# Banded attention inside a fused attention and feed-forward kernel: local scores of two heads in one product, against keys held with zeros for the other head

## The chip, the cores and the metric

The kernel runs on one core of one Trainium2 chip. TensorE (PE) multiplies matrices out of SBUF into PSUM banks; VectorE (DVE), ScalarE (ACT) and GpSimd (POOL) do elementwise work; SyncE (SP) issues most of the DMAs. The metric is the device time of one execution in microseconds (us); a median of several runs is given.

## What is computed

Two parts, one behind the other, all in float32:

```
# q, k, v: (8 batches, 8 heads, 576 tokens, 64)
pooled: q, k, v averaged over groups of 4 tokens -> 144 x 144 softmax attention, repeated 4 times
local:  softmax over |i - j| < 4 only          -> banded attention over 576 tokens
x = pooled + local, as (4608 tokens, 512)
h = x @ w_in                 # 512 -> 2048
out = (h * cos(h)) @ w_out   # 2048 -> 512
```

The weights come as float64 and are split on the chip into a high and a low part; so are x and h * cos(h). Three products (high-high, high-low, low-high) stand for one.

## The kernel before

**Attention units.** The work of one batch and one pair of heads is a unit: 8 batches by 4 pairs, 32 units. Its pieces are `u_qk` (loads q and k of two heads, 128 partitions = two heads by 64 dimensions, and sums groups of four tokens into `qkd` for the pooled part), `u_v` (loads and sums v), `u_s` (scores, softmax), `u_t` (transposes of the probabilities) and `u_pv` (probabilities times v; the result goes as `xs` into the tiles `x0h, x0l` to `x3h, x3l`). Batches 0 and 1 (`b < NEARLY`) run at the start while weights are split, the 24 units of batches 2 to 7 between the products of the feed-forward part.

**Local scores of a unit from batch 2 on (line 539).** Tokens are cut into 24 pieces of 24 queries; a piece meets 32 keys. 4 pieces lie on the four groups of 32 partitions of a PSUM bank, 6 such columns (`NSEG`) make a head. Each of the 48 products of a unit takes the 64 rows of one head (`hs`), 32 stationary columns of q and 32 moving columns of k, and one bank per head. In the profile each float32 product is two records, so L539 has 96 records a unit. The pooled scores (line 555, 8 records) follow in the same PE operation. Then come, on DVE, the mask (`band`, line 569), the maxima (574, 582), the subtractions (399, 585), on ACT the exponentials (605, 606), on DVE the sums (610), the reciprocals (612, 614) and the scaling (616, DVE or POOL).

**Moving probabilities (line 641).** DVE transposes the local probabilities in blocks (634); four DMAs on SP then move them into `ptb`, in which the other half of every 64 rows is zero, so that line 686 (24 products, 48 records) multiplies two pieces at once. Line 650 transposes the pooled probabilities on PE, 465 or 466 copies them into `ptd`, 667 multiplies them by v.

**Feed-forward.** A step is one tile of 384 tokens by one chunk of 128 hidden columns: `gemm1` (line 741, 12 matmuls), then on ACT and DVE h * cos(h) (750 to 759), and two steps later `gemm2` (line 777, 9 matmuls). There are 12 tiles by 16 chunks, 192 steps. Tiles 0 to 2 go in four blocks of four chunks (steps 0 to 47), tiles 3 to 11 one after the other; tile 3 (step 48) is the first that needs batch 2.

**Order.** Every operation is recorded with an estimated duration and what it reads and writes; a list scheduler (`Plan`) turns this into one fixed order per engine, which the engines then follow. A buffer that is used again is a ring: a later user waits for the earlier one. `dma` records a load with a planned latency of 1.8 us. `unit(last, step, ahead, ...)` places the pieces of a unit in recording order: `u_s` at `last`, `u_t` one `step` later, `u_pv` two. Where the planner sees PE idle in the first 300 us of its plan, it puts in products of an identity (line 916) that keep PE busy.

Of the kernel before, what the change touches and what calls it, by code (L numbers as in the profile page):

```python
# [300 lines left out]
def attn_ffn_kernel(ctx: ExitStack, tc: tile.TileContext, qT, kT, vdn, vl, w_in, w_out, out):  # L301
# [24 lines left out]
    band = const.tile([P, NSEG, BS], F32, name="band")  # L326
# [56 lines left out]
    def dma(nbytes, fn, r=(), w=(), pw=()):  # L383
        def begin():
            ins = fn()
            if ins is not None and len(begun) < FIRST:
                if len(begun) >= AHEAD:
                    tc.add_manual_dep(ins.ins, begun[-AHEAD].name, mybir.DependencyInfo(
                        mybir.DependencyClass.Sync, mybir.DependencyReason.DATA), reason="loads in flight")
                begun.append(ins.ins)  # L390
        o = pl.op("SP", max(0.45, nbytes / 262e3), begin, r=r, w=w, pw=pw, lat=1.8)
        loads.setdefault((pl.name,) + pl.arg, []).append(o)
        return o
# [52 lines left out]
    def ub(b, pr, name):  # L446
        shape, n, chunk, off = UNIT[name]
        if b == 1 and pr and name in "qk":

            own = cut(xx[1], 584 * (name == "k"), shape) if pr == 1 else \  # L450
                cut(wx[{(2, "q"): ("o", 8), (2, "k"): ("i", 7), (3, "q"): ("o", 7), (3, "k"): ("o", 6)}[(pr, name)]], 0, shape)
            return own
        if b < NEARLY and pr:
            return cut(wx[OWN[5 * (NPAIR - 1 - pr) + chunk]], off, shape)
        return sb({"ptl": "sml", "xs": "vd4"}.get(name, name), 2 if name == "ptl" else n, shape)
# [13 lines left out]
    def u_qk(b, pr):  # L469
# [4 lines left out]
        bk = bank(b, "t") if early and ON_PE else None  # L474
        for i, (src, ram) in enumerate(((q, qT), (k, kT))):
            dma(4 * P * SP_, lambda src=src, ram=ram: sp.dma_start(src.get(), ram[b, pr]), w=[src])
# [33 lines left out]
    def u_s(b, pr):  # L510
# [5 lines left out]
        if b == NEARLY and pr == 0:  # L516
            zeroed.extend((pl.buf(None), pl.buf(lambda: ptb, "ptb")))

            def zero():
                pool.tensor_copy(band, mask[:, 1:2].broadcast_to([P, NSEG, BS]))  # L520
                pool.memset(band[0:BS, 0, 0:PAD], NEG)
                pool.memset(band[P - BS:P, NSEG - 1, BQ + PAD:BS], NEG)
                pool.memset(ptb, 0.0)
            pl.op("POOL", 2.5, zero, w=zeroed)
# [6 lines left out]
        def l_mm():  # L531

            if b >= NEARLY:
                for f in range(2):
                    for n in range(NSEG):
                        for g in range(4):
                            h = (g // 2 + f) % 2
                            hs, o, c = slice(64 * h, 64 * h + 64), (4 * n + g) * BQ, LQ + BS * n
                            pe.matmul(banks[h].get()[BS * g:BS * (g + 1), c:c + BS],  # L539
                                      q.get()[hs, o:o + BS], k.get()[hs, o:o + BS], start=True, stop=True)  # L540
                return
# [17 lines left out]
        else:  # L559
            pl.op("PE", 1.55, lambda: (l_mm(), d_mm()), r=[q, k, qkd], pw=banks, w=loc + poo)  # L560
# [7 lines left out]
        for h in range(2):  # L568
            using(banks[h], pl.op("DVE", _dve(NSEG * BS), lambda h=h: dve.tensor_tensor(  # L569
                out=sml.get()[:, NSEG * h:NSEG * (h + 1)], in0=banks[h].get()[:, LQ:LQ + NSEG * BS].rearrange("p (s n) -> p s n", n=BS),  # L570
                in1=mask[:, h:h + NSEG] if b < NEARLY else band, op=ALU.add), r=[loc[h]] + zeroed[:1], pw=[sml]))
# [56 lines left out]
    def u_t(b, pr):  # L628
# [7 lines left out]
        if b >= NEARLY:  # L636
# [5 lines left out]
            dma(8 * P * NSEG * BS, move, r=[ptl], w=[u["ptb"]])  # L642
# [13 lines left out]
    def u_pv(b, pr):  # L656
# [24 lines left out]
        def w_mm():  # L681
            v4, pt = vt.get().rearrange("p a i n -> p (a i) n"), u["ptb"].get()
            for n in range(NSEG):
                for e, h in ((0, 0), (1, 1), (0, 1), (1, 0)):
                    r, o = slice(64 * e, 64 * e + 64), 2 * n * BQ
                    pe.matmul(banks[e].get()[64 * h:64 * h + 64, o:o + 2 * BQ], v4[r, NSEG * h + n, :],  # L686
                              pt[r, :, NSEG * h + n, :BQ], start=True, stop=True)
# [149 lines left out]
    for b in range(2, B):  # L837
        t0, t1 = tile_of(b * S), tile_of(b * S + S - 1)
        lo, hi = (done[t1 - NX] if t1 >= NX else 0), first[t0]
        for i in range(NPAIR):  # L840

            last = max(lo - 2.5 + (hi - lo - 1.0) * i / (NPAIR - 1), last + 1.5)
            unit(last, 1.4, 2.5, b, i)
# [116 lines left out]
```

## Time and profile before

| | |
|---|---|
| median of 3 runs | 1003.04 us (1002.43, 1003.04, 1006.76) |
| profiled execution, time / span | 1007.08 us / 1005.3 us |
| PE busy | 985.1 us, 98% of the span |
| DVE / ACT / POOL busy | 678.2 / 610.2 / 223.8 us |
| chain that ended last | PE 89%, DVE 5%, DMA 1% |
| granted PE clock, mean | 0.988 |

The busy times are shares of one profiled execution; which engine sets the end in which stretch is read from the windows and the chain, not from the totals. The profiled execution took 4.0 us more than the median of the runs.

### The profile page before, as it was taken

The page shows a single profiled execution, that of the slowest core. Times are in us where ns is not written, and L with a number is a line of the kernel's source. Part 1 is how long each engine was busy: PE and PEld are TensorE (multiplying, and loading weights), DVE is VectorE, ACT ScalarE, POOL GpSimd, SP SyncE. Part 2 cuts the span into 40 slices and gives each one's busy share as a digit, 9 for nine tenths or more (in the row PEclk, how much of TensorE's full clock was granted, in tenths as well). Part 3 has the DMA queues.
Part 4 walks back from the last instruction along what each step waited for, and adds up shares of the span by engine and source line. Part 5 has one row for each costly group of instructions (what it writes and reads, how often), then busy time and mean ns, then how long its engine had stood idle before and what let it go on. Part 6 is the DMA issues. An engine that isn't in the chain of part 4 may idle for free.

```text
span 1005.3 us, 23882 instructions
## 1 busy us (share of the span) xinstructions
PE 985.1 (98%) x9932; PEld 850.3 (85%) x9932; DVE 678.2 (67%) x1362; ACT 610.2 (61%) x1174; POOL 223.8 (22%) x280
## 2 busy tenths in 40 slices
PE   8898999999998999999999999999999999999998
PEld 5556898899886888889888888888888888899997
DVE  7699999985686678464758957655657765433433
ACT  4357688876665656555547746654646665655554
POOL 6685334631242203000002211200001300000000
PEclk9699999999999999999999999999999999999999
DMA  7874733332453422210212412201112320100000
GB/s 230 250 249 159 255 119 62 72 59 45 75 131 105 84 66 70 66 33 28 82 48 71 127 49 58 82 26 36 64 52 73 116 60 4 37 1 1 32 1 32
DMA packets 41051, 80.70 MB, mean 80 GB/s; under 512 B 4976, under 2 KB 16240, under 8 KB 40944
## 3 DMA queue, kind: packets, MB, share of 16 engines
q1 hardware_dynamic: 37056, 72.11, 23.2%
q0 software_dynamic: 3888, 7.08, 5.0%
q8 instruction: 78, 1.28, 0.5%
q14 instruction: 29, 0.24, 0.1%
HBM read 57.93 MB, written 16.52 MB: 74 GB/s over the span
## 4 chain that ended last, share of the span: by engine, by line
PE 89%; DVE 5%; DMA 1%; issue 1%; ACT 1%; POOL 1%; SPq 0%; ACTq 0%; POOLq 0%; DVEq 0%
PE bank L777 38%; PE bank L741 38%; PE bank L539 2%; PE bank L916 2%; PE bank L686 2%; PE bank L555 2%; PE bank L667 2%; PE bank L650 1%; DMA q<-qT 1%; PE bank L679 1%; DVE su L610 1%; DVE xxh L421 0%; DVE tr L756 0%; PE bank L546 0%; DVE xxh L425 0%
## 5 line engine op out<-in xcount | busy, mean ns | idle before, releaser
L777 PE MATMUL bank<-wo,gh 128*128 128x512 f32 x1152 | 363.9, 397 | 0.0
L777 PEld LDWEIGHTS bank<-wo,gh 128*128 128x128 f32 x1152 | 210.2, 188 | 38.1 <-issue 3.2
L777 PE MATMUL bank<-wo,gl 128*128 128x512 f32 x576 | 227.7, 396 | 0.0
L752 ACT ACTIVATE tr<-bank,bmagic 128x384 f32<-128x384 f32 x192 | 110.9, 578 | 114.1 <-PE bank L741 109.2
L756 DVE SCALAR_TENSOR_TENSOR tr<-tr,bank 128x384 f32<-128x384 f32 x192 | 105.0, 547 | 108.1 <-ACT tr L751 107.4
L753 DVE SCALAR_TENSOR_TENSOR tr<-tr,bank 128x384 f32<-128x384 f32 x192 | 105.7, 551 | 82.8 <-ACT tr L752 81.8
L750 ACT ACTIVATE tr<-tr 128x384 f32<-128x384 f32 x192 | 100.6, 524 | 77.0 <-DVE tr L753 76.4
L758 ACT ACTIVATE gh<-tr 128x384 fp32r<-128x384 f32 x163 | 85.3, 523 | 91.9 <-DVE tr L756 90.1
L399 DVE TENSOR_TENSOR gl<-tr,gh 128x384 fp32r<-128x384 f32 x154 | 91.7, 596 | 63.5 <-ACT gh L758 59.8
L777 PEld LDWEIGHTS bank<-wo,gl 128*128 128x128 f32 x576 | 108.1, 188 | 23.5
L741 PE MATMUL bank<-x3h,wi 128*128 128x384 f32 x384 | 106.9, 338 | 1.6 <-DVE tr L756 1.0
L741 PE MATMUL bank<-x0h,wi 128*128 128x384 f32 x384 | 107.0, 339 | 0.0
L741 PE MATMUL bank<-x1h,wi 128*128 128x384 f32 x384 | 107.0, 339 | 0.0
L741 PE MATMUL bank<-x2h,wi 128*128 128x384 f32 x384 | 106.8, 339 | 0.0
L751 ACT ACTIVATE tr<-tr 128x384 f32<-128x384 f32 x192 | 100.9, 525 | 6.1
L399 POOL TENSOR_TENSOR gl<-tr,gh 128x384 fp32r<-128x384 f32 x38 | 43.3, 1139 | 268.2 <-DVE gh L759 174.7
L741 PEld LDWEIGHTS bank<-x3h,wi 128*128 128x128 f32 x384 | 70.2, 188 | 4.3 <-DVE tr L756 1.5
L741 PEld LDWEIGHTS bank<-x0h,wi 128*128 128x128 f32 x384 | 70.2, 188 | 2.4 <-DVE wxo L569 0.2
L741 PEld LDWEIGHTS bank<-x1h,wi 128*128 128x128 f32 x384 | 70.2, 188 | 2.4 <-issue 0.4
L741 PEld LDWEIGHTS bank<-x2h,wi 128*128 128x128 f32 x384 | 70.2, 188 | 2.2 <-DVE xxh L425 0.2
L741 PE MATMUL bank<-x3l,wi 128*128 128x384 f32 x192 | 64.6, 336 | 0.1
L741 PE MATMUL bank<-x0l,wi 128*128 128x384 f32 x192 | 64.5, 336 | 0.0
(199 smaller groups left out, 1457.2 us busy)
## 6 DMA issues: line engine op xcount, KB each, us to landing
vl<-vl SPq DMA_DIRECT2D x26, 384.0 KB
out<-ob SPq DMA_DIRECT2D x36, 256.0 KB
wdi<-w_in SPq DMA_DIRECT2D x16, 512.0 KB
wdo<-w_out SPq DMA_DIRECT2D x16, 512.0 KB
q<-qT SPq DMA_DIRECT2D x26, 292.0 KB
k<-kT SPq DMA_DIRECT2D x26, 292.0 KB
vd<-vdn SPq DMA_DIRECT2D x26, 288.0 KB
out<-ob POOLq DMA_DIRECT2D x27, 256.0 KB, 5.3
```

The costliest lines, as they stand in the source:

```text
L399: f = lambda e: lambda: e.tensor_tensor(out=out(), in0=in0(), in1=in1(), op=ALU.subtract)
L539: pe.matmul(banks[h].get()[BS * g:BS * (g + 1), c:c + BS], q.get()[hs, o:o + BS], k.get()[hs, o:o + BS], start=True, stop=True)
L555: pe.matmul(banks[h].get()[:HD, i * SD:(i + 1) * SD], qkd.get()[hs, 0, i * HD:(i + 1) * HD], qkd.get()[hs, 1, :], start=True, stop=True)
L667: pe.matmul(banks[0].get()[64 * h:64 * h + 64, 2 * SD:3 * SD], vd.get()[:, kh, 64 * h:64 * h + 64], ptd.get()[:, h, kh, :], start=(kh == 0 ...
L741: pe.matmul(ph.get()[:, :m], w[:, i, kc, :], x[:, kc, :], start=(n == 0), stop=(n == 3 * KC - 1))
L750: act.activation(tr.get(), tr.get(), AF.Sin, scale=PI)
L751: return act.activation(tr.get(), tr.get(), AF.Square)
L752: pl.op("ACT", _act(m, True, 1), lambda: act.activation(tr.get(), h(), AF.Identity, bias=bmagic), r=[ph], w=[tr])
L753: pl.op("DVE", _dve(m), lambda: dve.scalar_tensor_tensor(out=tr.get(), in0=tr.get(), scalar=MAGIC, in1=h(), op0=ALU.subtract, op1=ALU.subt ...
L756: pl.op("DVE", _dve(m), lambda: dve.scalar_tensor_tensor(out=tr.get(), in0=tr.get(), scalar=0.5, in1=h(), op0=ALU.subtract, op1=ALU.mult), ...
L758: pl.op("ACT", _act(m, False), lambda: act.activation(gh.get(), tr.get(), AF.Copy), r=[tr], w=[gh], alts=[("DVE", _dve(m / 2), lambda: dve ...
L777: pe.matmul(o, (gh, gh, gl)[k].get()[:, sl], wo.get()[:, (0, 1, 0)[k]], start=(c == c0 and k == 0), stop=(c == c1 - 1 and k == 2))
```

## The change

From batch 2 on, k is loaded as two DMAs of 64 partitions into one constant buffer `kz` of two planes: plane 0 has head 0 in the upper 64 partitions and zeros below, plane 1 zeros above and head 1 below. POOL writes the zeros once. A product of line 560 takes all 128 rows of q (32 stationary columns) and 2 by 32 moving columns, one piece of both heads; there are 24 in a unit instead of 48, and the columns in PSUM run by piece and head instead of by head. `band` follows that order, with two more columns and as bfloat16, and line 707 (686 before) reads the probabilities by it. The sums of k in groups of four become two DVE operations of 64 partitions each, without POOL as an alternative. `ptd` now lies in the buffer of `smd`. In the planner, the move of the probabilities has a latency of 3.4 instead of 1.8 us, the score operation costs 1.3 instead of 1.55, units keep 2.25 instead of 1.5 steps of distance at least, and the pieces of a unit follow at 1.1 instead of 1.4 steps.

```diff
@@ constants
-    band = const.tile([P, NSEG, BS], F32, name="band")
+    band = const.tile([P, NSEG + 2, BS], BF16, name="band")
+    kz = const.tile([P, 2, SP_], F32, name="kz")
@@ ub: buffers of a unit
+        if name == "k" and (b >= NEARLY or not pr):
+            return pl.buf(lambda: kz if b >= NEARLY else kz[:, 0], "k.0")
...
-        return sb({"ptl": "sml", "xs": "vd4"}.get(name, name), 2 if name == "ptl" else n, shape)
+        return sb({"ptl": "sml", "xs": "vd4", "ptd": "smd"}.get(name, name), 2 if name == "ptl" else n, shape)
@@ u_qk
+        halves = [(slice(64 * h, 64 * h + 64), h) for h in range(2)]
+        def zero():
+            for hs, h in halves:
+                pool.memset(kz[hs, 1 - h], 0.0)
+        def load():
+            for hs, h in halves:
+                ins = sp.dma_start(kz[hs, h], kT[b, pr][hs])
+            return ins
+        def sums():
+            for hs, h in halves:
+                dve.tensor_reduce(out=qkd.get()[hs, 1], in_=kz[hs, h, PAD:PAD + S].rearrange("p (a r) -> p a r", r=4), axis=AX.X, op=ALU.add)
         for i, (src, ram) in enumerate(((q, qT), (k, kT))):
+            if i and not early:
+                if b == NEARLY and pr == 0:
+                    pl.op("POOL", 1.5, zero, w=[k])
+                dma(4 * P * SP_, load, pw=[k])
+                pl.op("DVE", 2 * _dve(S), sums, r=[k], pw=[qkd])
+                continue
@@ u_s
-                for f in range(2):
-                    for n in range(NSEG):
-                        for g in range(4):
-                            h = (g // 2 + f) % 2
-                            hs, o, c = slice(64 * h, 64 * h + 64), (4 * n + g) * BQ, LQ + BS * n
-                            pe.matmul(banks[h].get()[BS * g:BS * (g + 1), c:c + BS],
-                                      q.get()[hs, o:o + BS], k.get()[hs, o:o + BS], start=True, stop=True)
+                for n in range(NSEG):
+                    for g in range(4):
+                        o, c = (4 * n + g) * BQ, LQ + 2 * BS * (n % 3)
+                        pe.matmul(banks[n // 3].get()[BS * g:BS * (g + 1), c:c + 2 * BS].rearrange("p (h n) -> p h n", h=2),
+                                  q.get()[:, o:o + BS], k.get()[:, :, o:o + BS], start=True, stop=True)
-            pl.op("PE", 1.55, lambda: (l_mm(), d_mm()), r=[q, k, qkd], pw=banks, w=loc + poo)
+            pl.op("PE", 1.3, lambda: (l_mm(), d_mm()), r=[q, k, qkd], pw=banks, w=loc + poo)
...
-                in1=mask[:, h:h + NSEG] if b < NEARLY else band, op=ALU.add), r=[loc[h]] + zeroed[:1], pw=[sml]))
+                in1=mask[:, h:h + NSEG] if b < NEARLY else band[:, 2 * h:2 * h + NSEG], op=ALU.add), r=[loc[h]] + zeroed[:1], pw=[sml]))
@@ u_t, u_pv
-            dma(8 * P * NSEG * BS, move, r=[ptl], w=[u["ptb"]])
+            dma(8 * P * NSEG * BS, move, r=[ptl], w=[u["ptb"]], lat=3.4)
-                              pt[r, :, NSEG * h + n, :BQ], start=True, stop=True)
+                              pt[r, :, 2 * n + h, :BQ], start=True, stop=True)
@@ places of the units
-            last = max(lo - 2.5 + (hi - lo - 1.0) * i / (NPAIR - 1), last + 1.5)
-            unit(last, 1.4, 2.5, b, i)
+            last = max(lo - 2.5 + (hi - lo - 1.0) * i / (NPAIR - 1), last + 2.25)
+            unit(last, 1.1, 2.5, b, i)
```

Since the planner makes a new order, the line numbers move by 21 to 23 from `u_qk` on (741 is 762, 777 is 798, 916 is 937), and so do instructions on all engines. Three places show it.

On PE, where the feed-forward reaches tile 3 (the first matmul with `x3h`). Before, after the last product with v of batch 2 stand a whole step of tile 2 and its `gemm2`:

```order
L667 MATMUL bank<-ptd,vd 64x144 x4
L686 MATMUL bank<-ptb,vl 64x48 x24
L777 MATMUL bank<-wo_2992,gh 128x512 x2
...
L741 MATMUL bank<-x2h,wi_3176 128x384
...
L777 MATMUL bank<-wo_3090,gl 128x512
L741 MATMUL bank<-x3h,wi_932 128x384
```

Now the same product with v stands later, straight before tile 3, with six identity products (two of the twelve rows are shown) and the scores of the next unit between them:

```order
L798 MATMUL bank<-wo_2833,gl 128x512
L688 MATMUL bank<-smd,vd 64x144 x4
L707 MATMUL bank<-ptb,vl 64x48 x24
L937 LDWEIGHTS ident_b
L937 MATMUL bank<-ident_b 128x512
...
L560 MATMUL bank<-kz,q 32x64 x24
L576 MATMUL bank<-qkd 72x144 x4
L762 MATMUL bank<-x3h,wi_919 128x384
```

The last product with v of batch 2 moved from more than a step ahead of tile 3 to right ahead of it; two more identity products stand one step earlier.

On DVE at the same place, the first unit of batch 3: its mask (L569, L590), and the last unit of batch 2, whose result is added up by L698 (L719). Before:

```order
L569 TENSOR_TENSOR sml<-bank,band 128x192 x2
L582 TENSOR_REDUCE mxd<-bank 72x2
L574 TENSOR_REDUCE mxl<-sml 128x12
...
L490 TENSOR_REDUCE qkd<-q 128x144
L504 TENSOR_TENSOR vd_4137<-vd_4137 72x2x256
L505 TENSOR_TENSOR vd<-vd_4137 72x256
L466 TENSOR_SCALAR xd<-bank 128x144
L756 SCALAR_TENSOR_TENSOR tr<-tr,bank 128x384
L698 TENSOR_TENSOR vd_4248<-bank,xd 128x6x48
```

Now:

```order
L527 TENSOR_TENSOR vd_3890<-vd_3890 72x2x256
L528 TENSOR_TENSOR vd<-vd_3890 72x256
L719 TENSOR_TENSOR vd_4091<-bank,xd 128x6x48 x2
L400 TENSOR_TENSOR x3l<-vd_4091,x3h 128x384
L590 TENSOR_TENSOR sml<-bank,band 128x192 x2
...
L774 SCALAR_TENSOR_TENSOR tr<-tr,bank 128x384
L513 TENSOR_REDUCE qkd<-q 128x144
L491 TENSOR_REDUCE qkd<-kz 64x144 x2
L631 TENSOR_REDUCE su<-sml 128x12
```

The additions of the finished unit moved ahead of the next unit's mask, and the sums of q and k (now three operations) stand behind them, ahead of the softmax sums of the running unit.

On SP, the loads of the first unit of batch 3 (v is `vd_3893`, then `vd_3890`). Before:

```order
L641 DMA ptb<-sml 32x384 x4
L497 DMA vd_3893<-vdn 72x1024
L476 DMA q<-qT 128x584
L476 DMA k<-kT 128x584
L498 DMA vl<-vl 128x768
```

Now:

```order
L662 DMA ptb<-sml 32x384 x4
L521 DMA vl<-vl 128x768
L499 DMA q<-qT 128x584
L520 DMA vd_3890<-vdn 72x1024
L486 DMA kz<-kT 64x584 x2
```

k is two DMAs, and here they stand behind the load of v, which was ahead of q before.

More of the change, by code (lines that the diff above doesn't have):

```diff
@@ L381, in attn_ffn_kernel, with dma @@
     loads, begun = {}, []
-    def dma(nbytes, fn, r=(), w=(), pw=()):
+    def dma(nbytes, fn, r=(), w=(), pw=(), lat=1.8):
         def begin():
@@ L390, in begin @@
                 begun.append(ins.ins)
-        o = pl.op("SP", max(0.45, nbytes / 262e3), begin, r=r, w=w, pw=pw, lat=1.8)
+        o = pl.op("SP", max(0.45, nbytes / 262e3), begin, r=r, w=w, pw=pw, lat=lat)
         loads.setdefault((pl.name,) + pl.arg, []).append(o)
@@ L519, in zero @@
             def zero():
-                pool.tensor_copy(band, mask[:, 1:2].broadcast_to([P, NSEG, BS]))
-                pool.memset(band[0:BS, 0, 0:PAD], NEG)
-                pool.memset(band[P - BS:P, NSEG - 1, BQ + PAD:BS], NEG)
+                pool.tensor_copy(band, mask[:, 1:2].broadcast_to([P, NSEG + 2, BS]))
+                pool.memset(band[0:BS, 0:2, 0:PAD], NEG)
+                pool.memset(band[P - BS:P, NSEG:NSEG + 2, BQ + PAD:BS], NEG)
                 pool.memset(ptb, 0.0)
```

## The prediction

> **What bounds the kernel now.** I read the windows first, then the chain that ended last, then PE's timeline where PE is not full.
>
> ```profile
> 400.00:900.00 500.00, 500.00 (x4778) 442.21 (x4777) 316.01 (x654) 294.28 (x537) 54.91 (x69) 1.00 0.19 56
> 80.00:100.00 20.00, 17.07 (x365) 11.76 (x364) 20.00 (x42) 16.20 (x41) 10.87 (x10) 1.00 0.58 189
> 300.00:400.00 100.00, 95.88 (x1104) 82.16 (x1104) 71.17 (x154) 61.09 (x106) 23.51 (x30) 0.98 0.32 84
> 310.00:320.00 10.00, 8.02 (x130) 6.00 (x131) 7.75 (x18) 6.26 (x12) 3.36 (x5) 0.83 0.15 35
> ```
>
> Columns: stretch, length, busy time of PE, weight loads, DVE, ACT, POOL, then granted clock, DMA share, GB/s. From 400 to 900 us PE is busy all the time, DVE 316 of 500: there only PE's own work counts. From 80 to 100 DVE is full: the start hangs on DVE. Between 300 and 400 PE lacks 4.1 us, and a clock of 0.83 over 10 us costs 1.7 more. So three things can move the time: PE work per unit, the start, and the stretch at 300.
>
> The prices of PE's blocks, from the timeline (first two rows; the difference of the starts is the price, 0.95) and the chain (start, price, line, records):
>
> ```profile
> 436.05 1.02 PE L539 MATMUL bank<-k,q 64*32 64x32 f32 x96
> 437.00 0.47 PE L555 MATMUL bank<-qkd 64*72 64x144 f32 x4
> 451.04 0.64 PE bank L667 x8
> 451.68 0.84 PE bank L686 x48
> 494.27 0.50 PE bank L650 x8
> 36.05 1.52 PE bank L679 x96
> 482.97 0.64 PE bank L555 x8
> 479.91 2.11 PE bank L741 x12
> 477.82 2.08 PE bank L777 x9
> ```
>
> **The scores.** 24 units pay 0.95 us for L539; the new block has 48 records of 64 moving columns on four tiles of 128 rows by 32 columns, 12 records a tile. No row shows such a tile; I bound it by its neighbours. L650 streams 72 columns in 0.50/8 = 62 ns with its weight loads hidden, 0.87 ns a column, so 64 columns take 55 ns and 144 columns 125. L667 has 72 rows, thus all row groups but two column tiles, four records each: 4 x 125 = 0.50, and 0.14 is left for start and change. The new block is then 12 x 55 + 0.14 = 0.80 if the four tiles run side by side and loads hide. L686 has as many records on four tiles and takes 0.84: (0.84 - 0.14)/12 = 58 ns for 64 weight columns; L679, with 24 records a tile and the same 64, gives (1.52 - 0.14)/24 = 57, so these two are bound by weight loads; L539 uses four tiles at a time and gives (0.95 - 0.14)/24 = 34 for 32 columns. The load of 34 ns is thus under the stream of 55. I take 0.82, between 0.80 and 0.84: 24 x 0.13 = 3.1 us less. Ends: 3.6 less at 0.80; at the other end 12 more (below, rivals).
>
> The Trainium skill has a rule against this: its page "TensorE: Matmul & The Clock Gate" (Part 3: Packing small matmuls — row/col tiling) says that a weight load overlaps running matmuls only when their row groups differ, and the new tiles all hold every row group. The trace speaks against it: L667's 72-row tiles share the row groups too, and 0.64 us leaves no room for eight loads of 64 columns beside the streams. Its result is among the rivals, in a sentence of its own.
>
> **DVE, POOL and SP.** The sum of k is two operations:
>
> ```profile
> L490 DVE TENSOR_REDUCE qkd<-k 128x144 f32<-128x576 f32 x19 | 14.2, 745 | 1.5 <-DMA k<-kT 1.4
> DVE qkd L490 <- DMA q<-qT: 7.1, 4, 5.3
> 7.33 0.74 POOL ptb L523
> L569 DVE TENSOR_TENSOR sml<-bank,band 128x192 f32<-128x192 f32 x48 | 15.2, 350 | 6.3 <-PE bank L555 6.2
> 437.11 0.35 SPq L476 DMA_DIRECT2D q<-qT  x1
> ```
>
> 64 partitions cost what 128 do as long as columns set the time, so 24 x 0.745 = 18 us more on DVE, plus what POOL took of the sums of k. 15 of the units lie in 400 to 900, where DVE has 184 us free; if that cover is gone, it is late by 0.75 us a unit (a rival). Zeros on POOL: 2 x 584/768 x 0.74 = 1.1 us once, in a POOL queue far from full. The bfloat16 mask changes no count of operations: two of 350 ns a unit; between half and twice that DVE does 8 us less or 17 more, both inside its free time, so nothing. One DMA more per unit is 0.35 us of SP's queue. In the order it stands behind the load of q, in two places behind a load of v that waits for the previous result to be read; the sum of k waits then, and behind it on DVE the softmax sums of the running unit, then L650 on PE.
>
> How much slack a unit has (timeline and DMA queue; scores began at 436.05):
>
> ```profile
> 444.80 0.76 DVE L616 TENSOR_TENSOR smd<-smd,su 72x576 f32<-72x576 f32 x1
> 446.82 0.35 PE L650 MATMUL bank<-ident,smd 72*72 72x72 f32 x3
> 446.88 2.42 SPq L641 DMA_DIRECT2D ptb<-sml  x4
> 451.61 0.91 PE L686 MATMUL bank<-ptb,vl 64*64 64x48 f32 x48
> ```
>
> From the end of L539 (437.0) the pooled probabilities are ready at +8.5, PE wants them at +9.8; the moves are issued until +12.3, PE uses them at +14.6, unstalled. In the new order, with these block prices, the transposes of a unit stand 9.7 to 13.2 us behind its scores and L707 15.0 to 17.1. One sum more makes +9.3 out of +8.5: it fits, with 0.4 us left at the tightest unit. The moves have more room than before, so the PE waits for `ptb` go (in the order by 0.9 us in all, counted below). Unit after unit is now nearly serial, since `ptd` lies in `smd`: no next subtraction before L688 is done. In 18 units scores follow the last product by 1.4 to 6 us.
>
> **The start.** The first scores of batch 2 stand at step 4 now and at step 16 after.
>
> ```profile
> 103.29 1.25 PE L916 MATMUL bank<-ident_b 128*128 128x512 bf16 x5
> 106.14 0.47 PE L539 MATMUL bank<-k,q 64*32 64x32 f32 x33 [0.87 <-issue]
> 105.34 0.59 POOL L399 TENSOR_TENSOR x1l<-wxi,x1h 128x192 fp32r<-128x192 f32 x1 [3.03 <-ACT x1h L713]
> 107.18 0.44 PE L741 MATMUL bank<-x1h,wi 128*128 128x384 f32 x1
> ```
>
> Tile 1 is whole at 105.93, PE reaches it at 107.18 because of these scores. After, nine identity products (0.24 each: 1.25/5, less the overlap of the last record) stand there: PE arrives 1.2 to 1.4 us earlier, and pays 0.82 + 0.64 + 0.1 for the scores at step 16, where it is full. Net +0.2; DVE's other order in the first 100 us gives or takes up to 2.
>
> **Tile 3.** The stretch at 300 is the entry of batch 2 into the products.
>
> ```profile
> 300.30 6.73 DMA q<-qT
> 307.05 0.75 DVE qkd L490
> 308.50 0.60 DVE vd L505
> 309.11 0.22 DVE xd L466
> 309.79 0.37 DVE vd L698
> 300.39 0.71 PE L667 MATMUL bank<-ptd,vd 72*64 72x144 f32 x8
> 309.84 0.44 PE L741 MATMUL bank<-x3h,wi 128*128 128x384 f32 x1 [1.05 <-DVE tr L756]
> 312.25 0.45 PE L741 MATMUL bank<-x3h,wi 128*128 128x384 f32 x1 [0.56 <-ACT x3h L713]
> 324.44 0.73 PE L777 MATMUL bank<-wo,gh 128*128 128x512 f32 x2
> 334.95 0.91 PE L686 MATMUL bank<-ptb,vl 64*64 64x48 f32 x46 [0.17 <-DMA ptb<-sml]
> ```
>
> DVE waits in its queue for q of a later unit (6.73 us under way, 5.3 of them waited), and the additions of the finished unit (L466, L698) stand behind that. From 300.39 to 324.44 PE does three gemm1 (6.3), 27 matmuls of L777 (6.2), L650, L539, L555 once and L667, L686 twice (5.1): 17.6 of 24.05 us. 6.4 us are lost, some 0.5 of it the changes between blocks, and 0.5 more up to 335: 6.5 with the lower clock. In the new order the additions stand ahead of the sums of q and k, so this wait no longer holds them up; but the last unit of batch 2 stands later, right ahead of tile 3, with eight identity products, 8 x 0.24 = 1.9 us. What is late next is that unit's own chain, with the loads of the next one on the same busy DMAs: I take 2.0 us of new waits, between 0 and the old 6.5, nearer to 0 because the additions are free. -6.5 + 1.9 + 2.0 = -2.6; ends -4.6 and +1.9.
>
> **Sum.** -3.1 + 0.2 - 2.6 = -5.5 against the profiled 1007.08: 1001.6. The median is 4.0 lower. If that excess is the stall at tile 3, it is not to be had a second time and the median stays near 1001.5; if not, it is 997.5. I take the middle, 999.5.
>
> **Rivals.** (1) Serial units fall behind (slower): 18 units stand close to each other; if a sum of k is late by 0.75 us in each and the slack is used up, 13.5 us come on top: 1013. For it: one row shows 5.3 us of waiting for q on DVE, and k now lands last. Against: only four such waits after 105 us. It decides from 0.47 us a unit. (2) The four tiles don't overlap fully (slower): loads and streams of a tile in turns give 12 x (55 + 34) + 0.14 = 1.21 us, 24 x 0.26 = +6.2 instead of -3.1: 1008.8; two tiles at a time 24 x 55 + 0.14 = 1.46, +12.2: 1015. L667 speaks against both. By the skill's rule above, the first of these is what comes. (3) Tile 3 is as late as before: 4.5 us more, 1004. For it: the unit stands later and DMA is busy there. (4) The scores gain nothing, 0.95 remains because another limit holds L539: 1002.6; against it are the equal 57 ns of L679 and L686. (5) The new waits don't come and the start gains: 994.
>
> **Chances.** Forecast 0.40 (996 to 1003, its own range), of which 0.14 below 998.0; (5) 0.26; (3) 0.12; (4) 0.05; (2) 0.06, half of it for either way; (1) 0.11. A difference of 0.5%, 5 us, is about what a measurement of this kernel tells from none: faster 0.14 + 0.26 = 0.40, same 0.26 + 0.12 + 0.05 = 0.43, slower 0.17. Range 992 to 1009: outside are (1) and the tails of (2) and (5).
>
> **What would show it.** L560 at 0.80 to 0.84 us with 48 records; no wait of L762 on `x3h` over 1 us at 300 us and no lower clock there; a full PE from 400 to 900; DVE 10 to 14 us busier in that stretch; first tile-1 product near 106. Wrong if L560 is over 0.95, if L671 waits on `smd` unit after unit, or if the start shifts by several us.

## The result, and the profile after

The changed kernel takes 1010.99 us (median of 6 runs, 1008.6 to 1013.15), the kernel before 1004.08 us (median of 6, 1001.19 to 1006.76): a ratio of 1.0067, 95% interval 1.0045 to 1.0088. It is 7 us slower; 999.5 was forecast, 992 to 1009 as range. The profiled execution took 1010.47 us, its span is 1008.7.

The windows of the changed kernel, in the four stretches shown of before (us, then busy time of PE, weight loads, DVE, ACT, POOL, granted clock, DMA share, GB/s):

```profile
400.00:900.00 500.00, 498.47 (x4106) 437.88 (x4105) 334.44 (x688) 302.13 (x551) 34.40 (x48) 1.00 0.19 57
80.00:100.00 20.00, 16.92 (x402) 12.08 (x398) 19.43 (x40) 16.95 (x40) 10.76 (x12) 0.95 0.67 227
300.00:400.00 100.00, 96.71 (x927) 82.16 (x927) 75.64 (x157) 60.01 (x113) 14.40 (x20) 0.98 0.34 79
310.00:320.00 10.00, 9.55 (x97) 7.96 (x96) 9.11 (x19) 5.41 (x8) 1.62 (x2) 1.00 0.36 101
```

From 400 to 900 PE is no longer full (1.5 us missing), DVE has 18 us more to do (334 for 316) and POOL 20 less. The stretch at 310 is healed: 9.55 of 10 and a full clock, for 8.02 and 0.83 before. Yet 300 to 400 still lacks 3.3 us. The chain of the changed kernel gives the prices of the blocks, its waits say what PE waits for behind 330 us:

```profile
606.07 0.84 PE bank L707 x48
609.22 0.81 PE bank L560 x48
610.03 0.69 PE bank L576 x8
```

```profile
PE bank L671 <- DVE smd L637: 3.5, 3, 2.1
PE bank L762 <- DVE tr L777: 0.8, 2, 0.6
```

The new scores cost what was forecast: 0.81 us for 0.95. (L560, L576, L671, L688, L707, L762, L798 are the lines 539, 555, 650, 667, 686, 741, 777 of before; L491 is the sum of k, L513 that of q, L527 and L528 those of v, L590 the mask, L637 the scaling.) New is the wait of the transposes L671 for the scaled pooled probabilities; the kernel before has none there. Its longest, 2.10 us at 386, in the timelines of PE and of DVE:

```profile
383.58 0.40 PE L798 MATMUL bank<-wo,gl 128*128 128x512 f32 x1
386.08 0.67 PE L671 MATMUL bank<-ident,smd 72*72 72x72 f32 x8 [2.10 <-DVE smd L637]
387.38 0.45 PE L762 MATMUL bank<-x3h,wi 128*128 128x384 f32 x1 [0.63 <-DVE tr L777]
```

```profile
373.37 0.62 DVE L590 TENSOR_TENSOR sml<-bank,band 128x192 f32<-128x192 f32 x2 [0.27 <-PE bank L576]
...
376.75 0.74 DVE L513 TENSOR_REDUCE qkd<-q 128x144 f32<-128x576 f32 x1
377.41 0.35 DVE L780 CAST gh<-tr 128x384 fp32r<-128x384 f32 x1
379.05 0.69 DVE L527 TENSOR_TENSOR vd<-vd 72x512 f32<-72x512 f32 x1 [1.29 <-DMA vd<-vdn]
379.78 0.42 DVE L528 TENSOR_TENSOR vd<-vd 72x256 f32<-72x256 f32 x1
380.12 1.52 DVE L491 TENSOR_REDUCE qkd<-kz 64x144 f32<-64x576 f32 x2
...
383.63 0.67 DVE L527 TENSOR_TENSOR vd<-vd 72x512 f32<-72x512 f32 x1
384.33 0.94 DVE L528 TENSOR_TENSOR vd<-vd 72x256 f32<-72x256 f32 x1
385.19 0.74 DVE L637 TENSOR_TENSOR smd<-smd,su 72x576 f32<-72x576 f32 x1
```

From the mask to the end of the scaling (373.37 to 385.93) 12.6 us pass on DVE. Over the units between 330 and 900 us this stretch takes 9.6 us in the mean, here the longest; in e16 below, 8.5 us in the mean and 9.4 at most. Sums for other units stand in between: one of q, two of k, two of v, and a wait of 1.29 for a load. Behind the wait the clock is halved from 387.97 to 391.38, another 1.7 us. The same place in one window, of the changed kernel and then of the kernel before in its third trace (e16 below):

```profile
380.00:392.00 12.00, 9.26 (x44) 8.19 (x43) 9.45 (x19) 5.66 (x10) 1.24 (x2) 0.86 0.15 41
```

```profile
380.00:392.00 12.00, 12.00 (x206) 10.20 (x205) 10.72 (x25) 8.56 (x16) 2.54 (x4) 1.00 0.34 101
```

At the start PE reaches tile 1 at 106.77 us, and step 1 waits for POOL, whose queue has the zeros of `kz` straight ahead of the split of the first weights (timelines of PE and POOL):

```profile
65.85 1.01 PE L762 MATMUL bank<-x0h,wi 128*128 128x384 f32 x2 [4.33 <-POOL wi L400]
```

```profile
62.08 1.05 POOL L528 TENSOR_TENSOR wxo<-wxi 72x256 f32<-72x256 f32 x1
63.08 1.38 POOL L482 MEMSET kz<- 64x584 f32 x2
64.53 1.26 POOL L400 TENSOR_TENSOR wi<-xxh,wi 128x512 fp32r<-128x512 f32 x1
```

### The profile page after: what moved, and what is told of

Same layout as the page of the kernel before. It is cut to its first block, busy times and chain, and to the rows that moved or that the text cites. A ratio compares the mean times of both kernels' runs of the same rounds, so it can differ in the third digit from the quotient of the medians.

```text
span 1008.7 us, 21657 instructions
## 1 busy us (share of the span) xinstructions
PE 984.5 (98%) x8780; PEld 844.6 (84%) x8780; DVE 705.9 (70%) x1400; ACT 615.0 (61%) x1193; POOL 183.0 (18%) x236
## 4 chain that ended last, share of the span: by engine, by line
PE 79%; DVE 8%; DMA 4%; ACT 3%; POOL 3%; issue 2%; ACTq 0%; DVEq 0%; POOLq 0%
PE bank L762 36%; PE bank L798 35%; PE bank L707 2%; PE bank L560 2%; PE bank L688 2%; PE bank L576 1%; DMA wdi<-w_in 1%; PE bank L671 1%; DMA q<-qT 1%; DVE tr L777 1%; DVE tr L774 1%; ACT tr L771 1%; DVE xxh L428 1%; DMA vd<-vdn 1%; DVE su L631 1%
## 5 line engine op out<-in xcount | busy, mean ns | idle before, releaser
L798 PE MATMUL bank<-wo,gh 128*128 128x512 f32 x1152 | 362.2, 395 | 0.3 <-ACT ob L814 0.3
L798 PEld LDWEIGHTS bank<-wo,gh 128*128 128x128 f32 x1152 | 211.2, 188 | 38.8 <-issue 3.8
L798 PE MATMUL bank<-wo,gl 128*128 128x512 f32 x576 | 227.8, 396 | 0.0
L777 DVE SCALAR_TENSOR_TENSOR tr<-tr,bank 128x384 f32<-128x384 f32 x192 | 105.0, 547 | 114.6 <-ACT tr L772 114.1
L400 DVE TENSOR_TENSOR gl<-tr,gh 128x384 fp32r<-128x384 f32 x150 | 86.6, 577 | 61.5 <-ACT gh L779 56.8
L798 PEld LDWEIGHTS bank<-wo,gl 128*128 128x128 f32 x576 | 108.0, 188 | 23.6 <-DVE gl L400 0.3
L779 ACT ACTIVATE gh<-tr 128x384 fp32r<-128x384 f32 x157 | 82.1, 523 | 72.5 <-DVE tr L777 70.8
L762 PE MATMUL bank<-x0h,wi 128*128 128x384 f32 x384 | 108.9, 344 | 4.3 <-POOL wi L400 4.3
L762 PE MATMUL bank<-x3h,wi 128*128 128x384 f32 x384 | 108.0, 342 | 0.7 <-DVE tr L777 0.6
L762 PE MATMUL bank<-x1h,wi 128*128 128x384 f32 x384 | 108.2, 342 | 0.1
L762 PE MATMUL bank<-x2h,wi 128*128 128x384 f32 x384 | 107.2, 340 | 0.2 <-DVE tr L777 0.2
L400 POOL TENSOR_TENSOR gl<-tr,gh 128x384 fp32r<-128x384 f32 x42 | 47.8, 1138 | 288.9 <-DVE gh L780 144.6
L762 PEld LDWEIGHTS bank<-x0h,wi 128*128 128x128 f32 x384 | 71.1, 190 | 8.4 <-POOL wi L400 4.7
L762 PEld LDWEIGHTS bank<-x3h,wi 128*128 128x128 f32 x384 | 70.9, 190 | 3.7 <-DVE tr L777 1.4
L762 PEld LDWEIGHTS bank<-x1h,wi 128*128 128x128 f32 x384 | 70.6, 189 | 3.4 <-PE bank L937 1.0
L762 PEld LDWEIGHTS bank<-x2h,wi 128*128 128x128 f32 x384 | 70.2, 188 | 2.5 <-DVE tr L777 0.6
L762 PE MATMUL bank<-x0l,wi 128*128 128x384 f32 x192 | 65.1, 339 | 0.0
L762 PE MATMUL bank<-x3l,wi 128*128 128x384 f32 x192 | 65.0, 339 | 0.0
```

The source lines that it names most:

```text
L400: f = lambda e: lambda: e.tensor_tensor(out=out(), in0=in0(), in1=in1(), op=ALU.subtract)
L762: pe.matmul(ph.get()[:, :m], w[:, i, kc, :], x[:, kc, :], start=(n == 0), stop=(n == 3 * KC - 1))
L777: pl.op("DVE", _dve(m), lambda: dve.scalar_tensor_tensor(out=tr.get(), in0=tr.get(), scalar=0.5, in1=h(), op0=ALU.subtract, op1=ALU.mult), ...
L779: pl.op("ACT", _act(m, False), lambda: act.activation(gh.get(), tr.get(), AF.Copy), r=[tr], w=[gh], alts=[("DVE", _dve(m / 2), lambda: dve ...
L798: pe.matmul(o, (gh, gh, gl)[k].get()[:, sl], wo.get()[:, (0, 1, 0)[k]], start=(c == c0 and k == 0), stop=(c == c1 - 1 and k == 2))
```

## The experiments

First theory: the zeros on POOL and the throttled start cost some us, and the two sums of k with those of v fill DVE inside a unit. Rivals: units in series (the schedule) cost by themselves; the identity products at tile 3; the loads of v. Each timed kernel ran beside the kernel before on the same chip. The table collects all of them: median, ratio to before with its interval, and from the profiled execution the first product of tile 1 and all that PE waited between 330 and 990 us.

| run | what | median us | ratio [95%] | tile 1 at | PE waits 330-990 |
|---|---|---|---|---|---|
| | before, three traces | 1003.2 to 1004.6 | 1 | 107.2, 106.1, 106.1 | 0.4, 0, 0 |
| | changed | 1010.99 | 1.0067 [1.0045, 1.0088] | 106.8 | 4.3 |
| e1 | schedule alone, old products | 1009.2 | 1.0054 [1.0033, 1.0075] | 109.6 | 0.8 |
| e6 | landing 3.4 alone, old products | 1011.32 | 1.0081 [1.0054, 1.0109] | 110.7 | 0 |
| e7 | spacing alone, old products | 1010.84 | 1.0069 [1.0046, 1.0092] | 113.1 | 0.7 |
| e9 | before, the planner's ninth order | 1003.45 | 0.9980 [0.9956, 1.0004] | 108.4 | 0 |
| e2 | changed, no identity products at tile 3 | 1011.2 | 1.0073 [1.0045, 1.0101] | 107.7 | 4.4 |
| e3 | changed, zeros on DVE | 1009.97 | 1.0061 [1.0039, 1.0084] | 101.8 | 5.0 |
| e4 | changed, v of batches 2 to 7 on POOL | 1010.42 | 1.0064 [1.0038, 1.0090] | 111.5 | 1.7 |
| e8 | e3 and e4 | 1007.37 | 1.0026 [1.0004, 1.0048] | 105.6 | 2.3 |
| e10 | changed, 29th order | 1008.29 | 1.0042 [1.0021, 1.0063] | 107.3 | 3.8 |
| e11 | changed, 18th order | 1006.9 | 1.0033 [1.0014, 1.0052] | 107.4 | 3.8 |
| e12 | changed, one head to a product | 1013.9 | 1.0095 [1.0068, 1.0122] | 106.4 | 4.1 |
| e13 | changed, v of four units on POOL | 1007.09 | 1.0037 [1.0019, 1.0055] | 103.8 | 2.7 |
| e14 | e11 and e13 | 1008.07 | 1.0045 [1.0029, 1.0061] | 109.2 | 4.4 |
| e15 | new products, units as before | 1009.63 | 1.0068 [1.0043, 1.0093] | 105.9 | 3.3 |
| e17 | changed, second sum of k on POOL | 1004.91 | 1.0006 [0.9986, 1.0027] | 105.8 | 1.0 |
| e18 | e17 and e13 | 1005.66 | 1.0015 [0.9991, 1.0038] | 103.3 | 1.0 |

### e1, e6, e7: the schedule without the products

e1 is the kernel before with what the change does to the schedule, but for the planned price of the score block:

```diff
-        return sb({"ptl": "sml", "xs": "vd4"}.get(name, name), ...
+        return sb({"ptl": "sml", "xs": "vd4", "ptd": "smd"}.get(name, name), ...
-            dma(8 * P * NSEG * BS, move, r=[ptl], w=[u["ptb"]])
+            dma(8 * P * NSEG * BS, move, r=[ptl], w=[u["ptb"]], lat=3.4)
-            last = max(..., last + 1.5)
-            unit(last, 1.4, 2.5, b, i)
+            last = max(..., last + 2.25)
+            unit(last, 1.1, 2.5, b, i)
```

e6 has its second pair of lines alone, e7 its third.

> The kernel before with the schedule's part of the change alone: landing 3.4, units 2.25 apart with steps of 1.1, ptd in smd; scores, keys, sums and mask as before. First theory (the two sums of k and the zeros are what costs: DVE is too full inside a unit, POOL too late at the start): without them tile 3 keeps its gain of 4 us and no long wait of the transposes on smd is left, 1000 to 1004. Rival (units in series cost by themselves, whatever the products are): 1008 to 1013, and the transposes wait on smd as in the changed kernel.

> The kernel before with the landing of the moves planned at 3.4 us instead of 1.8 and nothing else. Theory now (the units' distance and the shared buffer, which put the units in series, cost the 5 us of the schedule): no change, 1002 to 1006. Rival (the later landing is what spoils the start's order): 1008 to 1010.

> The kernel before with the units 2.25 apart and steps of 1.1 and nothing else: ptd in its own buffer, landing 1.8. Theory now (units in series cost): 1007 to 1010, a late start or waits at steps 47 to 72. Rival (the shared buffer of ptd and smd is what costs): 1001 to 1005, tile 3 without the old 7 us.

All three are 5 to 8 us slower than before, so neither the landing nor the spacing is the one culprit, and the first theory's 1000 to 1004 for e1 falls. But the rival's mark is missing too: behind 330 us the transposes never wait (0 to 0.8 us in all, none of it on `smd`). More than half of their loss lies ahead of that, in the start: tile 1 comes 2.4 to 5.9 us later than in the first trace of before, whose DVE is mostly full there, and against the third trace (e16) they are 4.4, 4.7 and 8.0 us late at step 5, 7.6, 9.1 and 9.9 at step 188. In e6 DVE stood 6.0 us behind one result of ACT and 2.8 behind another (waits of DVE, 40 to 112 us); the kernel before, third trace, stood 4.7 at its longest:

```profile
DVE xxh L421 <- ACT xxh L420: 6.0, 1, 6.0
DVE wi L399 <- ACT wi L431: 2.8, 1, 2.8
```

```profile
DVE wxi L698 <- ACT wxi L465: 4.7, 1, 4.7
```

### e9, e10, e11: the same work in another order

The planner makes eight passes and keeps the order that it rates best. More passes give another order of the same instructions:

```diff
-CFG = dict(cold=6.8, queue=0.0, alttol=0.3, iters=8, ...
+CFG = dict(cold=6.8, queue=0.0, alttol=0.3, iters=9, ...
```

e9 is this in the kernel before; e10 and e11 have 32 and 18 in the changed kernel, and differ from it ahead of step 36 alone.

> The kernel before with nine passes of the planner instead of eight: it then takes its ninth order, with the same instructions, which differs from the eighth up to step 48 alone. Theory now (the start hangs on which wait stands at the head of DVE's queue, so each order of it costs its own few us, and the order of before is a good one): 1006 to 1011, the first product of tile 1 at 109 to 112 us instead of 106 to 107. Rival (the start is bound by the amount of work, not its order; what was slow in the three kernels with the old products was their schedule after step 40): 1002 to 1005.

> The changed kernel with 32 passes of the planner, which then takes its 29th order: the same from step 36 on, another start, and the scores of the first unit of batch 2 at step 4, ahead of tile 1, where they are free. Theory now: 1.6 us less for those scores, and a start that is its own draw, anywhere from 5 us earlier to 4 later than in the changed kernel: 1004 to 1013. Rival (start bound by work): 1009.4.

> The changed kernel with 18 passes of the planner, its 18th order: the same from step 36 on, a third start, scores of the first unit at step 4. Theory now: as for the run before, and not the same time as it. Rival (start bound by work): 1009.4, the same in both.

e9 is as fast as before (the interval holds 1), so it is not true that any other order of that start costs: my theory was too strong. e10 and e11 give 2.5 and 3.4 us of the changed kernel's loss back (1.0067 to 1.0042 and 1.0033; the intervals overlap). In the traces step 36 comes 1.6 and 2.0 us earlier than in the changed kernel, and nearly all of that would be the scores of the first unit (1.6: 0.81, 0.69 and the change between blocks), which stand at step 4 there, ahead of tile 1; step 5 itself comes at the same time in all three (111.6 to 111.7 us). What e11 gains beyond that lies behind step 36, where the order is the same: it has no half clock there. So in these traces the two other orders of the start won 2 us and no more. The waits behind 330 us stay nearly as they were (3.8).

### e5, e16: the kernel before, traced again

Nothing is edited; two more traces of the same instructions.

> The kernel before, unchanged, for a second trace of it: its first profiled execution lay 3 us above its median. If the wait for q at tile 3 (6.73 us under way) was what lay above it, this one shows 1003 to 1004 and a loss at tile 3 of 3 to 4 us instead of 7.6; if the start is what varies, tile 1 comes earlier than 107.2 us and tile 3 loses 7 us as before.

> The kernel before, unchanged, a third trace of it. If the loss at tile 3 (7.6 us in the first, 2.9 in the second) is an accident of the first: 2.5 to 3.5 here. If it comes and goes: anywhere between.

Both took 1001.06 us. Before's window from 300 to 325 us, in its first trace and in the third:

```profile
300.00:325.00 25.00, 21.25 (x288) 16.72 (x288) 15.84 (x36) 13.82 (x23) 8.06 (x11) 0.93 0.39 105
```

```profile
300.00:325.00 25.00, 23.74 (x314) 20.21 (x312) 20.22 (x44) 17.82 (x30) 10.57 (x15) 1.00 0.50 127
```

From the start of step 47 to that of step 52 PE took 33.5 us in the first trace, 29.1 and 28.7 in the others, with the same instructions. Each block of PE set against its usual price, the first lost an estimated 7.6 us there and the others about 3 each; DVE waited 5.3 us at a time for q in the first, 2.3 and 2.6 in the others. The stall that the prediction meant to win back at tile 3 was mostly an accident of one execution.

### e2: the identity products at tile 3

```diff
-           fgap=0.4, f0=0.8, fend=300.0, warm=0, fill=0.8)
+           fgap=0.4, f0=0.8, fend=200.0, warm=0, fill=0.8)
```

> The changed kernel without the identity products at tile 3 (none after 200 us of the plan), the order of everything else unchanged. First theory: they are 1.9 us of PE's time that nothing hides and the clock holds without them, 1009.0. Rival (they keep the clock up): a half clock of 3.4 us comes back at 310, 1.7 us lost, 1010.5 to 1012.

The time is that of the changed kernel (1.0073 for 1.0067). Without them PE waits 1.9 us for L719 at the same place, and a half clock comes back from 313.0 to 316.4: the rival. They fill a wait and cost nothing.

### e3, e4, e8: zeros and sums of v elsewhere

```diff
-                pool.memset(kz[hs, 1 - h], 0.0)
+                dve.memset(kz[hs, 1 - h], 0.0)
...
-        pl.op("POOL", 2.2, v_add(pool), ..., alts=[("DVE", 1.1, v_add(dve))], shares=True)
+        pl.op("POOL", 2.2, v_add(pool), ..., alts=[("DVE", 1.1, v_add(dve))] if b < NEARLY else [], shares=True)
```

e3 is the first pair of lines (and the operation planned on DVE at 0.7 us), e4 the second, e8 both.

> The changed kernel with the zeros of kz written by DVE instead of POOL; the order from step 16 on is unchanged. First theory: POOL's split of the first weights (1.4 us behind the zeros) comes earlier, PE's wait of 4.3 us at step 1 shrinks to 3, but tile 1 hangs on DVE, which gets 0.7 us more: 1009.5 to 1011.5. Rival (the zeros on POOL are the whole loss of the start): first product of tile 1 at 104 to 105 us, 1008 to 1009.

> The changed kernel with the sums of v of batches 2 to 7 on POOL alone, so that no sum of v stands between mask and scaling of a unit on DVE. First theory: the waits of the transposes on smd at 382 (2.1 us), 619 (1.1) and the half clock behind the first (1.7) go, 1005 to 1007. Rival (the waits come from late loads or from the two sums of k alone): waits on smd stay or the products with v wait for POOL, 1010 to 1012.

> The changed kernel with the zeros on DVE and the sums of v of batches 2 to 7 on POOL. If the start of the one (3.5 us earlier than before at step 5) and the missing waits of the other (3 to 4 us) add up: 1004 to 1006. If each new order shuffles the start by some us in either direction, whatever the edit: the waits at 382 and 619 are gone, the first product at step 5 lies anywhere from -4 to +4 us of before, 1006 to 1012.

e3: tile 1 comes 5 us earlier, and the time is only 1 us less, within the interval. Of the 5 us 3.7 are left at step 5 and 2.6 at step 47; behind it, with waits of 5.0 us and two half clocks at 386 and 622, 2.1 more are lost. e4: no wait on `smd` is left behind 330, but tile 1 comes 4.7 us later, so the time says nothing; e8, with both, gains 4 us. Here the planner moves too much with each edit for one cause to be seen.

### e12: one head to a product

```diff
-                    for g in range(4):
-                        pe.matmul(banks[n // 3]...[.., c:c + 2 * BS], q.get()[:, o:o + BS], k.get()[:, :, o:o + BS], ...)
+                    for h in range(2):
+                        for g in range(4):
+                            pe.matmul(banks[n // 3]...[.., c:c + BS], q.get()[:, o:o + BS], k.get()[:, h, o:o + BS], ...)
```

> The changed kernel in its own order, but each head's scores as a product of its own (96 records of 32 moving columns on the same four tiles of 128 rows). If the gain comes from the number of loads (34 ns each, 24 to a tile): L560 back at 0.95 us, 1014.4. If the four full-height tiles as such are faster: 0.81 as now, 1011.

The timeline of PE gives the block as the difference of the starts, 0.96 us:

```profile
440.08 1.03 PE L561 MATMUL bank<-kz,q 128*32 128x32 f32 x96
441.04 0.71 PE L577 MATMUL bank<-qkd 64*72 64x144 f32 x8
```

The ratio rises from 1.0067 to 1.0095, 2.8 us, where 24 x (0.96 - 0.81) = 3.6 were to be expected; the intervals hold that. So it is the two heads in one product, with half the weight loads, that gains, not the tall tiles as such. In the trace, in which every other instruction keeps its order, step 188 starts 4.0 us later: what the scores save arrives in the time.

### e13, e14: the sums of v of four units

The units at steps 60 and 108 are those whose chain on DVE holds sums of v. Taking only these off leaves all of PE's instructions, and nearly all of the others, in their order:

```diff
-        ... alts=[("DVE", 1.1, v_add(dve))], shares=True)
+        ... alts=[("DVE", 1.1, v_add(dve))] if (b, pr) not in ((4, 0), (4, 1), (6, 0), (6, 1)) else [], shares=True)
```

e14 has it with the 18th order of e11.

> The changed kernel with the sums of v of four units alone (the first two each of batches 4 and 6) on POOL; every other instruction keeps its place, so that only the units at steps 60 and 108 have no sum of v between mask and scaling on DVE. Theory: the waits at 382 and 619 shrink from 2.1 and 1.1 to under 0.8 us, the half clock at 388 goes, 1006.5 to 1008.5. Rival (the two sums of k alone overfill DVE there): waits over 1.2 us stay, 1010 to 1011.

> Both together: the 18th order's start and those four sums of v on POOL. If the two losses are separate: 1006.9 less 3 to 4, 1002.5 to 1004.5, level with the kernel before. Rival (as for the run before): 1006 to 1007.

e13 is 3 us faster than the changed kernel (the intervals just overlap) and has no half clock behind 330, but waits of 1.2 us stay at both places. Its profiled execution was the fastest of twelve (1003.79); its step 188 comes 6.1 us earlier than in the changed kernel, of which 3.1 are there at step 47 already, with the same order of PE: that part is chance. At the second place the path from mask to scaling did not get shorter at all (11.7 us for 11.6), because the additions, now on POOL, stretch the DVE instructions beside them. `L633`, 0.16 us in the changed kernel, takes 0.95, and the scaling of `sml`, 0.56 there, 0.88:

```profile
612.99 1.29 POOL L527 TENSOR_TENSOR vd<-vd 72x512 f32<-72x512 f32 x1 [3.22 <-DMA vd<-vdn]
614.36 0.74 POOL L528 TENSOR_TENSOR vd<-vd 72x256 f32<-72x256 f32 x1
```

```profile
613.36 0.95 DVE L633 TENSOR_SCALAR su<-su 128x16 f32<-128x16 f32 x1
614.35 0.25 DVE L635 RECIPROCAL su<-su 128x16 f32<-128x16 f32 x1
614.63 0.88 DVE L637 TENSOR_TENSOR sml<-sml,su 128x384 f32<-128x384 f32 x1
```

e14 did not add up: 4.1 us of waits on `smd`, and 1008. The sums of v are part of it, not the whole.

### e15: the products with the units of before

The changed kernel with the three edits of e1 taken back, so that units overlap as before and `ptd` has its own buffer; three buffers `tr` instead of four make the room, and `iters=32`.

> The new products, keys and sums with the units of before: 1.5 apart, steps of 1.4, landing 1.8, ptd in a buffer of its own; room for it is made with three buffers for tr instead of four, and the planner takes its 31st order of 32. Theory (units in series are what makes DVE too full; the scores' gain is real): no waits over 0.6 us of the transposes on smd after step 52, 3.5 us gained there, a start within 3 us either way: 998 to 1004. Rival (the second sum of k is too much in either schedule): waits at steps 65 and 97, 1006 to 1010.

The theory of units in series falls: the transposes at 401 have waited 1.9 us here too, with a half clock at 402, and the time is that of the changed kernel. PE also loses some 4 us more than before in steps 5 to 47 (an estimate by the usual prices), and three buffers `tr` may cost of themselves; that was not separated.

### e17, e18: the second sum of k off DVE

```diff
+        def sums1():
+            o, x = qkd.get()[64:128, 1], kz[64:128, 1, PAD:PAD + S].rearrange("p (a r) -> p a r", r=4)
+            pool.tensor_tensor(out=o, in0=x[:, :, 0], in1=x[:, :, 1], op=ALU.add)
+            for r in (2, 3):
+                pool.tensor_tensor(out=o, in0=o, in1=x[:, :, r], op=ALU.add)
-                pl.op("DVE", 2 * _dve(S), sums, r=[k], pw=[qkd])
+                pl.op("DVE", _dve(S), lambda: sums(0), r=[k], pw=[qkd])
+                pl.op("POOL", 3 * _pool(SD), sums1, r=[k], pw=[qkd])
```

e18 adds the edit of e13.

> The changed kernel with the second of the two sums of k made on POOL (three additions of 64x144), so that each unit has one sum of k on DVE as before. Theory (the second sum is what overfills the units): the transposes wait on smd under 0.8 us everywhere after step 52 and the half clock at 388 goes, 3 to 4 us less than the changed kernel but for the start, which is a new draw of up to 3 us either way: 1004 to 1010, middle 1007. Rival (POOL's additions stretch DVE's instructions by as much, or the units in series are too tight anyway): waits over 1.2 us stay, 1009 to 1012.

> As the run before, and the sums of v of the four units of e13 on POOL too. Theory: no wait of the transposes over 0.5 us after step 52, 1003 to 1009, and 0 to 1 us under the run before, since the start is the same. Rival: as there.

e17 is level with before (1.0006, interval 0.9986 to 1.0027): of the changed kernel's 1.0067 nothing is left that can be told from noise. PE's waits from 330 to 990 us, all there are (L678 is the transposes here, L769 gemm1), and its windows from 380 to 392 and from 400 to 900:

```profile
PE bank L678 <- DVE smd L644: 0.8, 2, 0.6
PE bank L769 <- DVE tr L784: 0.2, 1, 0.2
```

```profile
380.00:392.00 12.00, 11.82 (x65) 10.32 (x64) 10.49 (x21) 6.82 (x13) 4.45 (x7) 1.00 0.17 49
400.00:900.00 500.00, 500.00 (x4069) 439.92 (x4068) 328.50 (x678) 302.05 (x548) 63.35 (x92) 1.00 0.20 57
```

Waits of 4.3 us and the half clock of 1.7 are down to 1.0; PE is full again. The longest path from mask to scaling falls from 12.6 to 11.0 us, and at the second place, with one sum of v in both, from 11.6 to 10.1; the mean only from 9.6 to 9.4, since the planner put other work in. At the first place one sum of v and the wait for its load went out as well, so e17 doesn't price the second sum of k alone. Tile 1 comes 0.9 us earlier as well. In the two traces step 188 comes 3.4 us earlier than in the changed kernel: 1.5 us are won by step 16, 1.1 lost by step 47 and 3.1 won behind it. The rest of the 6 us between the two medians no trace shows. Over all traces the last column of the table divides by one thing: with the old products, in five orders, 0 to 0.8 us; with both sums of k on DVE 3.3 to 5.0 (1.7 to 2.7 where sums of v were taken off, but for e14); with one of them on POOL 1.0. e18 adds nothing to it. No version beat the kernel before by more than the interval.

## Why the prediction was wrong, point by point

**Tile 3, the first step that failed.** "6.4 us are lost" was read from one execution, and "6.5 with the lower clock" put into the sum as if every run had it. (The trace has 24 matmuls of L777 in that stretch and not 27, so it lost 7.1 there.) Two more traces lose about 3. The changed kernel loses an estimated 1.6 and pays 1.9 for identity products: 3.5 us. That is 4 less than the first trace, where 2.6 less was forecast, but half a us or so more than the other two. So against what the kernel before usually takes, the term is near +0.5 instead of -2.6. The prediction saw the profiled run 4.0 above the median and asked whether the stall was that excess, then took the middle of the two answers; the answer was nearly all of it, and this cost the forecast 2.0 us. That the additions no longer wait for q, and the full clock at 310, came as said.

**DVE, the second.** "One sum more makes +9.3 out of +8.5: it fits, with 0.4 us left at the tightest unit." The sums were costed by count (0.745 each), hidden under DVE's share of the whole stretch. In the trace a unit's path on DVE also holds the sum of q, the sums of v of other units, and a load that one of them waits for: 12.6 us at 373. The stretch grew by 1.1 us in the mean (8.5 to 9.6), and two units went over 11 us. Rival (1), a sum of k that makes the units late, came nearest, with too small a chance (0.11), and its spread was wrong: not 0.75 us in 18 units, but 2.1, 1.1 and 0.2 in three, 0.8 more at gemm1 behind them, and a half clock behind the longest. Its reason, units in series, was wrong too: e15 has the waits without them. That the waits on `smd` go or shrink when the longest of these paths gets shorter is shown by e4, e17 and e18 (10.5 to 11.0 us); how much of it is the second sum of k, how much the sums of v and the wait for a load, is open.

**The start, the third.** "+0.2, +-2": PE was to come to tile 1 1.2 to 1.4 us earlier. It came 0.4 earlier than in the trace shown, 0.7 later than in the other two, and the scores at step 16 cost their 1.6 in full. At step 16 the changed kernel is 1.9 us behind the first trace of before (159.4 for 157.5) and 3.0 behind the third (156.4), so the term was 2 to 3 us too small. Two other orders of the same start win 1.6 and 2.0 us of that by step 36. The zeros on POOL, costed at nothing, do stand ahead of the split for which PE waits 4.3 us. e3 moves them and reaches tile 1 5 us earlier, but with a new order of the start, so their own share is open.

**The scores were right.** 0.82 was forecast, 0.81 measured: 24 x 0.145 = 3.5 us for 3.1. The four tiles of 128 rows run side by side: rival (2), loads and streams in turns at 1.21 us, did not come. e12 turns the gain off. (The 994 of rival (5) does not follow from the terms: without the 2.0 us of new waits, and with 2 won at the start, the forecast becomes 995.5.)

**The sum.** Step 188 of the changed kernel's profile starts 8.8 us later than in e16, an execution 3.1 us faster than the median of its kernel. Of this 1.3 are there at step 5. Behind it, each block of PE set against its usual price (estimates, each good to some half a us): the scores -1.9 (3.3 gained in 23 units, 1.45 for the unit that no longer stands ahead of tile 1), other losses up to step 47 +2.0, tile 3 +0.5, steps 52 to 72 +5.1, steps 72 to 188 +2.3: 9.3 in all for 8.8, so the whole is known to about a us. The 7.4 behind step 52 hold the waits of 4.3 and the half clock of 1.7; the rest of them has no wait to its name. The scores' gain came as forecast and was paid back twice, in DVE's queue and at the start.

**Open.** How much of the 7 us is the start and how much the waits differs from run to run: one order's tile 1 came at 106.8, 107.7 and 103.8 us in three traces (the changed kernel, e2, e13). Why e14 does not add up is not settled, nor why the landing alone (e6) makes the kernel 8 us slower while another order of the start (e9) costs nothing.

## What to carry to other kernels

An engine that is two thirds busy can still be full on the path that matters: count what stands in its queue between the two ends of a dependency, with the work of other units in it, before an added operation is called hidden. A stall read from one trace is a gain only if a second trace has it; trace the kernel twice, or compare its time with the median, before it goes into a sum. Where a planner redraws the order, run the schedule's part and the arithmetic's part apart: here the schedule alone (e1) and the arithmetic alone (e15, with a buffer less) each cost 5 us or more, at different places.

## What the runs showed of the hardware

A short wait can cost a half clock. PE waited 2.10 and 0.63 us between 384 and 387 us, and the clock was halved for 3.41 us from 387.97. The Trainium skill ("TensorE: Matmul & The Clock Gate", HAM oscillation — how this bites in real kernels) gives idle gaps over some 3.4 us as what to avoid; here the two gaps came to 2.7 us in all, so the trace goes further than the rule. In e10 a single wait of 1.62 us, ended at 618.7, was followed by a half clock from 619.4. Yet the length alone does not decide it: e11 waited 2.00 and 0.63 us at the same place, e2 1.93 and 0.63, and neither had a half clock there; nor had e13, with waits of 1.2. So a half clock of 1.7 us more or less between two traces can be chance.

DVE stretches beside POOL. The same instruction, usually 0.42 us, takes 1.51 when it meets a running addition of POOL (timeline of e3):

```profile
60.68 1.59 POOL L527 TENSOR_TENSOR wxi<-wxi 72x512 f32<-72x512 f32 x1
...
61.06 1.51 DVE L422 TENSOR_SCALAR xxh<-xxh 128x512 f32<-128x512 f32 x1
```

The Trainium skill ("SBUF — State Buffer", Who interferes with whom) says that such an instruction and one of POOL hold a pair of ports in turns, each for its whole length; the DVE instruction ends at 62.57, 0.30 after POOL's and 0.12 earlier than 0.42 us behind it would be, so the trace roughly agrees. So a sum moved to POOL can cost DVE what it saves, as the second place of e13 shows. In e17 it did not do so in full: POOL's three additions took 0.57 us each as a rule, and from 400 to 900 us DVE is busy 5.9 us less than in the changed kernel (328.5 for 334.4), where the 15 sums taken off it were 11.2; the planner moved other work as well, so what the stretching took of the difference is open.
